# One-token attention and GeGLU on one core: TensorE's repeated halves as loops, and one chunk of rows dealt unevenly to the DMA engines

## The chip, the cores and the metric

The kernel runs on one core of a Trainium2 chip. The metric is device time in microseconds; lower is better.

## The reference

One decode step of a transformer block in float32: eight sequences, one new token each, model width 1024, 32 query heads of 128 on 4 key/value heads, a window of the last 1024 cached positions, and a gated MLP of width 3584.

```python
h  = x + attention(layernorm(x))          # q = x@wq; softmax(q k^T / sqrt(128)) v; @wo
g  = layernorm(h) @ w_gate                # [8, 3584]
u  = layernorm(h) @ w_up
h2 = h + (gelu(g) * u) @ w_down           # w_down is [3584, 1024]
```

Every weight and every cached key and value is used once, so nearly all of the 111 MB read are these.

## The kernel before

The weights go through one tile in on-chip memory, `w`, which has 2 x 16384 floats on each of 128 partitions: two halves of 8.39 MB (`HALF`, `PLACE`). They were laid out on the host in the order of use, one contiguous row for each partition and load. Only SyncE's queue loads them (`load`): each load waits on a semaphore until TensorE's last product has read the half that it overwrites, and while one half is being used the other is being filled. So the order of the loads is the order of the work: wq in two halves, k in two, v in two, wo in two, then w_gate and w_up (a first pair with four column blocks of 512, a second pair with three), then w_down.

Each stage multiplies by 32-column stationary tiles, so four products stand side by side in TensorE's four column groups. The activations are spread over the partitions for this, and VectorE transposes them between the stages.

- Attention: scores for both halves of heads first (L204), each with its softmax (L211 to L218) into tiles of its own; then, for each half, the transposes of the probabilities (L240), the product with v (L254) and the sum over the heads' own columns (L261, L264). `heads_out` turns this into the operand of wo (L225, L228).
- wo gives y (L281), which is folded by a product with `add2` (L291) and added to x (L296).
- Gate and up (L310), GELU (L334), product (L336), and a transposition into `at_`: on VectorE for the first 16 row blocks (L338), on TensorE for the other 12 (L342, L345).
- w_down: 28 rows of 128 x 1024, a row being 0.5 MB. They come in chunks of `DN_PARTS` rows (8, 8, 4, 4, 2, 1), and the last row in two parts (192 and 64 columns of each quarter). Rows 0 to 25 go into one accumulator (L364), on two column groups up to row `SLOW` and then on four. VectorE copies this out as `d1` (L371). Row 26 (L378), `d1` folded by `add2` (L384) and the parts of row 27 (L391) are summed in two more accumulators, and two additions with `h_sb` (L401, L404) give the output, which two DMAs store.

The chip has 16 DMA engines, and a load of 128 partitions is spread over all. The last part of row 27 is loaded as 100, 20 and 8 partitions (`SHARES`), so that some engines carry more of it than others.

Of the kernel before, what the change touches and what calls it, by code (L numbers as in the profile page):

```python
# [8 lines left out]
P = 128  # L9
# [17 lines left out]
ROUND = 3 * N * NC  # L27
PLACE = [0, HALF] * 5 + [0, ROUND]
DN_PARTS = (8, 8, 4, 4, 2, 1)
DN_AT = (2 * ROUND, 0, 8 * D, ROUND, ROUND + 4 * D, ROUND + 6 * D)  # L30

SHARES = ((0, 100), (100, 120), (120, 128))
LAST_AT = ROUND + 7 * D

SLOW = 20

# [41 lines left out]
def decode_block(nc, out, x, srcs, W):  # L78
# [13 lines left out]
    s_load = [nc.alloc_semaphore(f"s_load{i}") for i in range(len(srcs))]  # L92
    s_fin = nc.alloc_semaphore("s_fin")
# [5 lines left out]
    loaded[-1] = (s_load[-1], 16 * len(SHARES))  # L99
# [19 lines left out]
    qz = [sb(f"qz{hf}", [P, 2, 10 * 32]) for hf in range(2)]  # L119
    ot = sb("ot", [P, HQ, 32])  # L120
    for a in (*qz, ot):
        t_zero = pool(lambda e: e.memset(a, 0.0))
# [14 lines left out]
    def layernorm_t(src, name, *deps):  # L137
# [26 lines left out]
        t = dve(lambda e: e.transpose(xt.rearrange("p c m -> p (c m)"), xn), t)  # L164
        return xt, t
# [14 lines left out]
    for hf in range(2):  # L180
        load(2 + hf, PLACE[hf], HALF, t_q[hf])
    for hf in range(2):
        q_sb = sb(f"q{hf}", [P, N])
        t = dve(lambda e: e.tensor_scalar(q_sb, bank(4 + hf), scale, None, op0=ALU.mult), t_q[hf])  # L184
        qt = sb(f"qt{hf}", [P, N])
        t = dve(lambda e: e.transpose(qt, q_sb), t)
        for s in range(2):
            last = dve(lambda e: e.tensor_copy(
                qz[hf][:, s].rearrange("p (b m) -> p b m", b=B)[:, :, 0:REP],
                qt.rearrange("p (s k b r) -> p s b k r", s=2, k=REP, r=4)[:, s, :, :, 0]), t, t_zero)  # L190
        t_qz.append(last)


    t_s, t_p, share, t_share = [], [], [], []
    p_sb = [sb(f"p{hf}", [P, W]) for hf in range(2)]
    for hf in range(2):
        s_ps = bank(2 * hf, 2)
        k_t = w[:, hf * HALF:(hf + 1) * HALF].rearrange("p (s b k) -> p s b k", s=2, b=B)
        for b in range(HB):
            for k0 in range(0, W, N):  # L200
                for r in range(NQ):
                    s, half = divmod(r, 2)
                    at = 32 * b + 160 * half
                    ins = pe(lambda e: e.matmul(  # L204
                        s_ps[32 * r:32 * r + 32, k0:k0 + N], qz[hf][:, s, at:at + 32],
                        k_t[:, s, half * HB + b, k0:k0 + N],
                        start=(b == 0), stop=(b == HB - 1)), loaded[2 + hf], t_qz[hf], inc=False)
        t_s.append(pe.mark(ins))
        load(4 + hf, PLACE[hf], HALF, t_s[hf])
        nmax = sb(f"nmax{hf}", [P, 1])  # L210
        t = dve(lambda e: e.tensor_reduce(out=nmax, in_=s_ps, axis=AX.X, op=ALU.max, negate=True), t_s[hf])  # L211
        tot = sb(f"tot{hf}", [P, 1])
        t = act(lambda e: e.activation(p_sb[hf], s_ps, AF.Exp, bias=nmax, accum_out=tot), t)  # L213
        t_p.append(t)
        rtot = sb(f"rtot{hf}", [P, 1])
        t = dve(lambda e: e.reciprocal(rtot, tot), t)
        share.append(sb(f"share{hf}", [P, HB]))
        t_share.append(dve(lambda e: e.tensor_scalar(share[hf], own, rtot, None, op0=ALU.mult), t, t_own))  # L218


    t_o, o_sb, t_osb, t_ot = [], [], [], [None, None]

    def heads_out(hf, b, *deps):
        op = bank(b)[:, 0:P]
        t = pe(lambda e: e.transpose(op, o_sb[hf], ident), t_osb[hf], t_id, *deps)  # L225
# [6 lines left out]
    free = [None, None]  # L232
    for hf in range(2):
        pt = sb(f"pt{hf}", [P, KC, P])
        t_pt = []
        for h in range(2):
            pp = bank(6 + h).rearrange("p (c m) -> p c m", m=P)
            for i in range(KC // 2):
                c = h * KC // 2 + i
                ins = pe(lambda e: e.transpose(pp[:, i], p_sb[hf][:, c * P:(c + 1) * P], ident),  # L240
                         t_p[hf], t_id, free[h], inc=False)
            t = pe.mark(ins)
            dst = pt[:, h * KC // 2:(h + 1) * KC // 2, :]
            if h == 0:
                free[h] = dve(lambda e: e.tensor_copy(dst, pp), t)
            else:
                free[h] = act(lambda e: e.copy(dst, pp), t)
            t_pt.append(free[h])
        v_t = w[:, hf * HALF:(hf + 1) * HALF].rearrange("p (s c b d) -> p s c b d", s=2, c=KC, b=B)
        o_ps = bank(4 + hf)  # L250
        for c in range(KC):
            for r in range(NQ):
                s, half = divmod(r, 2)
                ins = pe(lambda e: e.matmul(  # L254
                    o_ps[32 * r:32 * r + 32, :], pt[:, c, 32 * r:32 * r + 32],
                    v_t[:, s, c, half * HB:(half + 1) * HB, :],
                    start=(c == 0), stop=(c == KC - 1)), loaded[4 + hf], t_pt[2 * c // KC], t_qz[hf], inc=False)
        t_o.append(pe.mark(ins))
        load(6 + hf, PLACE[hf], HALF, t_o[hf])
        o_sb.append(sb(f"o{hf}", [P, DH]))  # L260
        t = dve(lambda e: e.tensor_scalar(  # L261
            o_sb[hf], o_ps[:, 0:DH], share[hf][:, 0:1], None, op0=ALU.mult), t_o[hf], t_share[hf])
        for b in range(1, HB):
            t = dve(lambda e: e.scalar_tensor_tensor(  # L264
                o_sb[hf], o_ps[:, b * DH:(b + 1) * DH], share[hf][:, b:b + 1], o_sb[hf],
                op0=ALU.mult, op1=ALU.add), t)
        t_osb.append(t)
        if hf == 1:
            heads_out(0, 6, *free)
# [4 lines left out]
    for hf in range(2):  # L274
        if hf == 1:
            heads_out(1, 7, *free)
        for h in range(0, 2 * REP, 2):
            for r in range(NQ):
# [5 lines left out]
                    loaded[6 + hf], t_ot[hf], t_p[0], inc=False)  # L284
        t_y.append(pe.mark(ins))
        load(8 + hf, PLACE[hf], HALF, t_y[hf])
# [10 lines left out]
    ht, t_ht = layernorm_t(h_sb, "ln2", t_h)  # L297
# [3 lines left out]
    t_at = []  # L301
    for k, nb in enumerate((NQ, DF // N - NQ)):
        pair = bank(2 + 2 * k, 2)
        t_g = []
        for s in range(2):
            i = 8 + 2 * k + s
            for c in range(NC):
                for j in range(nb):
                    at = PLACE[i] + (c * nb + j) * N
                    ins = pe(lambda e: e.matmul(  # L310
                        pair[32 * j:32 * j + 32, s * N:(s + 1) * N], ht[:, c], w[:, at:at + N],
                        start=(c == 0), stop=(c == NC - 1)), loaded[i], t_ht, t_p[1], t_osb[1], inc=False)
                if k == 0 and s == 1 and c == NC // 2 - 1:
                    t_half = pe.mark(ins)
            t_g.append(pe.mark(ins))
            if k == 0 and s == 0:
                load(10, PLACE[10], ROUND, t_g[0])
            elif k == 0:
                load(11, PLACE[11], ROUND, t_half)
                load(12, DN_AT[0], DN_PARTS[0] * D, t_g[1])  # L320
            elif s == 0:
                for i in range(1, 3):
                    load(12 + i, DN_AT[i], DN_PARTS[i] * D, t_g[0])
            else:
                for i in range(3, len(DN_PARTS)):
                    load(12 + i, DN_AT[i], DN_PARTS[i] * D, t_g[1])
                load(tail, LAST_AT, NQ * CUT)
                at = LAST_AT + NQ * CUT
                for p0, p1 in SHARES:
                    nc.sync.dma_start(w[p0:p1, at:at + D - NQ * CUT], srcs[tail + 1][p0:p1]).then_inc(  # L330
                        s_load[tail + 1], 16)
        rows = 32 * nb
        ge = sb(f"ge{k}", [P, N])
        t = act(lambda e: e.activation(ge[:rows], pair[:rows, 0:N], AF.Gelu_apprx_tanh), t_g[0])  # L334
        hm = sb(f"hm{k}", [P, N])
        t = dve(lambda e: e.tensor_mul(hm[:rows], ge[:rows], pair[:rows, N:2 * N]), t, t_g[1])  # L336
        if k == 0:
            t_at.append(dve(lambda e: e.transpose(at_[:, 0:16, :].rearrange("p c m -> p (c m)"), hm), t))  # L338
        else:
            hp = bank(6)[:, 0:4 * rows].rearrange("p (i m) -> p i m", i=4)  # L340
            for i in range(4):
                ins = pe(lambda e: e.transpose(hp[:, i], hm[:rows, i * P:(i + 1) * P], ident[:rows, :rows]),  # L342
                         t, t_ot[0], inc=False)
            t = pe.mark(ins)
            t_at.append(dve(lambda e: e.tensor_copy(  # L345
# [139 lines left out]
```

## Time and profile before

| | |
|---|---|
| median of 3 runs | 265.94 us (265.69 to 267.08) |
| the profiled execution | 265.95 us, span 264.6 us |
| TensorE busy | 137.1 us (52%) |
| VectorE, ScalarE busy | 24.2 us, 10.2 us |
| read from HBM | 111.18 MB, 421 GB/s over the span |
| code packets of TensorE's queue | 7 of 16 KB |

The span runs from the first instruction to the last; the measured time has 1.35 us around it. Lines are L with a number of the kernel before. PE is TensorE's products, PEld its weight loads, DVE VectorE, ACT ScalarE, SP SyncE. In the timeline a row has its start, its length, the engine, the line, the operation with what it writes and reads, a count, and in brackets how long the engine had been idle and for what. In the chain a row has start, length and what ran. In the windows, the columns are the stretch, its length, busy time and count of each engine, the granted TensorE clock, the share of the 16 DMA engines that was busy, and GB/s. "instruction" in the DMA rows is code that an engine's sequencer fetches through the same DMA engines.

### The profile page before, as it was taken

To read this page: it belongs to the slowest core of one execution; us is meant where nothing else is said; L and a number is where in the kernel's file an instruction comes from. 1 tells how busy PE (TensorE), PEld (TensorE's weight loads), DVE (VectorE), ACT (ScalarE), POOL (GpSimd) and SP (SyncE) were. 2 spreads that over 40 slices of the span, in tenths; PEclk is the share of its full clock that TensorE was granted. 3 is DMA by queue.
4 is the path that set the end of the run, shared out by engine and by line. 5 is a ranking of instruction groups with operands and counts; after the bars stand their busy time and mean duration, and the time that the engine had idled before them with its cause. 6 is when DMAs were issued, how large, how long until landed. Compare 5 with 4: busy or idle time off the path is not lost.

```text
span 264.6 us, 1990 instructions
## 1 busy us (share of the span) xinstructions
PE 137.1 (52%) x918; PEld 38.1 (14%) x918; DVE 24.2 (9%) x74; ACT 10.2 (4%) x14; POOL 2.7 (1%) x9
## 2 busy tenths in 40 slices
PE   0005706705806906807707708509409485689795
PEld 0001201101201301202102102102102021122131
DVE  1050200200110020300200000330000200010001
ACT  1020000000010020110000000020000000000000
POOL 4000000000000000000000000000000000000000
PEclk9999975955965895965975956956965959599999
DMA  8997999899999999998999899989999999999994
GB/s 317 480 466 327 475 475 428 367 466 475 406 396 466 468 396 416 456 475 357 448 457 456 367 446 458 456 386 436 458 411 446 394 468 411 423 421 411 426 417 135
DMA packets 3236, 111.44 MB, mean 421 GB/s; under 512 B 508, under 2 KB 796, under 8 KB 1052
## 3 DMA queue, kind: packets, MB, share of 16 engines
q1 hardware_dynamic: 3036, 111.25, 97.8%
q8 instruction: 7, 0.11, 0.2%
q10 hardware_dynamic: 192, 0.07, 0.1%
q14 instruction: 1, 0.01, 0.0%
HBM read 111.18 MB, written 0.13 MB: 421 GB/s over the span
## 4 chain that ended last, share of the span: by engine, by line
DMA 78%; PE 21%; SPq 0%; issue 0%; DVE 0%
DMA w<-weights 78%; PE banks L310 6%; PE banks L204 4%; PE banks L175 4%; PE banks L254 4%; PE banks L281 3%; SPq L104 0%; PE banks L378 0%; PE banks L384 0%; PE banks L391 0%; DVE o_fin L401 0%; DVE o_fin L404 0%; PE banks L225 0%
## 5 line engine op out<-in xcount | busy, mean ns | idle before, releaser
L310 PE MATMUL banks<-w,ln_t 128*32 128x512 f32 x224 | 37.4, 751 | 29.2 <-DMA w<-weights 29.2
L175 PE MATMUL banks<-w,ln_t 128*32 128x512 f32 x128 | 18.2, 734 | 33.2 <-DMA w<-weights 33.2
L204 PE MATMUL banks<-w,qz 128*32 128x512 f32 x128 | 19.3, 770 | 21.2 <-DMA w<-weights 21.2
L281 PE MATMUL banks<-w,ot 128*32 128x512 f32 x128 | 18.4, 741 | 19.2 <-DMA w<-weights 19.2
L254 PE MATMUL banks<-w,pt 128*32 128x512 f32 x128 | 18.0, 727 | 18.1 <-DMA w<-weights 18.1
L364 PE MATMUL banks<-w,at 128*32 128x512 f32 x104 | 20.3, 595 | 2.2 <-DMA w<-weights 2.1
L310 PEld LDWEIGHTS banks<-w,ln_t 128*32 128x32 f32 x224 | 9.2, 134 | 56.9 <-issue 34.2
L175 PEld LDWEIGHTS banks<-w,ln_t 128*32 128x32 f32 x128 | 4.7, 132 | 45.8 <-issue 34.5
L204 PEld LDWEIGHTS banks<-w,qz 128*32 128x32 f32 x128 | 5.3, 137 | 35.2 <-issue 35.2
L281 PEld LDWEIGHTS banks<-w,ot 128*32 128x32 f32 x128 | 5.0, 132 | 31.2 <-issue 31.2
L254 PEld LDWEIGHTS banks<-w,pt 128*32 128x32 f32 x128 | 4.9, 131 | 29.8 <-issue 29.8
L364 PEld LDWEIGHTS banks<-w,at 128*32 128x32 f32 x104 | 5.3, 109 | 16.5 <-issue 12.3
L336 DVE TENSOR_TENSOR hm<-ge,banks 128x512 f32<-128x512 f32 (+1 forms) x2 | 1.4, 686 | 60.3 <-PE banks L310 60.3
L211 DVE TENSOR_REDUCE nmax<-banks 128x1 f32<-128x1024 f32 x2 | 2.5, 1225 | 35.7 <-PE banks L204 35.7
L213 ACT ACTIVATE p<-banks,nmax 128x1024 f32<-128x1024 f32 x2 | 2.2, 1114 | 75.8 <-DVE nmax L211 75.8
L184 DVE TENSOR_SCALAR q<-banks 128x512 f32<-128x512 f32 x2 | 1.4, 692 | 32.3 <-PE banks L175 32.3
L261 DVE TENSOR_SCALAR o<-banks,share 128x128 f32<-128x128 f32 x2 | 0.7, 351 | 32.6 <-PE banks L254 32.6
L148 ACT ACTIVATE ln_sd<-ln_ve 32x1 f32<-32x1 f32 x2 | 0.4, 202 | 70.5 <-DVE ln_ve L146 70.5
L334 ACT ACTIVATE ge<-banks 128x512 f32<-128x512 f32 (+1 forms) x2 | 1.2, 595 | 48.2 <-PE banks L310 48.2
L371 DVE COPY d<-banks 128x512 f32<-128x512 f32 x1 | 0.7, 692 | 22.0 <-PE banks L364 22.0
L148 ACT ACT_TABLE_LOAD x2 | 2.6, 1283 | 1.7 <-DVE add L125 1.7
L228 DVE COPY ot<-banks 128x64 f32<-128x64 f32 x4 | 0.8, 262 | 18.4 <-PE banks L225 18.4
(55 smaller groups left out, 34.2 us busy)
## 6 DMA issues: line engine op xcount, KB each, us to landing
w<-weights SPq DMA_DIRECT2D x2, 6144.0 KB, 23.5
w<-weights SPq DMA_DIRECT2D x2, 4096.0 KB, 26.7
w<-weights SPq DMA_DIRECT2D x2, 2048.0 KB, 24.6
w<-weights SPq DMA_DIRECT2D x1, 1024.0 KB, 22.3
w<-weights SPq DMA_DIRECT2D x1, 512.0 KB, 23.6
w<-weights SPq DMA_DIRECT2D x1, 384.0 KB, 24.0
w<-weights SPq DMA_DIRECT2D x10, 29.6
w<-weights SPq DMA_DIRECT2D x1, 100.0 KB
```

Of the source, the lines that this page charges most:

```text
L148: t = act(lambda e: e.activation(sd, ve, AF.Sqrt), t_ve)
L175: ins = pe(lambda e: e.matmul(q_ps[32 * j:32 * j + 32, :], xt[:, c], w[:, hf * HALF + c * SET + j * N:hf * HALF + c * SET + (j + 1) * N], ...
L184: t = dve(lambda e: e.tensor_scalar(q_sb, bank(4 + hf), scale, None, op0=ALU.mult), t_q[hf])
L204: ins = pe(lambda e: e.matmul(s_ps[32 * r:32 * r + 32, k0:k0 + N], qz[hf][:, s, at:at + 32], k_t[:, s, half * HB + b, k0:k0 + N], start=(b ...
L211: t = dve(lambda e: e.tensor_reduce(out=nmax, in_=s_ps, axis=AX.X, op=ALU.max, negate=True), t_s[hf])
L213: t = act(lambda e: e.activation(p_sb[hf], s_ps, AF.Exp, bias=nmax, accum_out=tot), t)
L254: ins = pe(lambda e: e.matmul(o_ps[32 * r:32 * r + 32, :], pt[:, c, 32 * r:32 * r + 32], v_t[:, s, c, half * HB:(half + 1) * HB, :], start ...
L281: ins = pe(lambda e: e.matmul(y_ps[32 * r:32 * r + 32, :], ot[:, 2 * hf * REP + h + e_], w[:, at:at + N], start=(hf == 0 and h == 0), stop ...
L310: ins = pe(lambda e: e.matmul(pair[32 * j:32 * j + 32, s * N:(s + 1) * N], ht[:, c], w[:, at:at + N], start=(c == 0), stop=(c == NC - 1)), ...
L334: t = act(lambda e: e.activation(ge[:rows], pair[:rows, 0:N], AF.Gelu_apprx_tanh), t_g[0])
L336: t = dve(lambda e: e.tensor_mul(hm[:rows], ge[:rows], pair[:rows, N:2 * N]), t, t_g[1])
L364: ins = pe(lambda e: e.matmul(d1_ps[32 * r:32 * r + 32, :], at_[:, q, :], w[:, at:at + N], start=(r not in started), stop=(q >= pairs - 2) ...
```

## The change

1. On TensorE, attention becomes a loop that runs twice over one piece of code (`nc.Fori` on that engine alone): scores, transposes, product with v. The order of the loads becomes k, v, k, v. Semaphores that the loop waits on are counted down by each wait (`take`), and the tiles `qz`, `p`, `pt` and the accumulators exist once in place of twice. `heads_out` for both halves follows behind the loop.
2. Gate and up likewise: two rounds with four column blocks of 448 each (`M`, `SIDE`). VectorE does both transpositions.
3. w_down's chunks are 8, 8, 4, 3, 1, 2, 1 rows. The chunk of one row (`SHARED`, row 23) is loaded by three DMAs over 32, 60 and 36 partitions, whose source has an outer dimension of 16, 10 and 9: nine engines get 12 rows of 4 KB, one 8 and six 2. The last part of row 27 is one load.
4. The tail: `d1` holds rows 0 to 23 (`QUADS`); `d1`, folded, and rows 24 to 26 are summed in one accumulator, which VectorE adds to `h_sb` as `pre`; row 27's parts have accumulators of their own, added to `pre`.
5. Behind TensorE's last product stand two instruction blocks, each aligned to 256 instructions and holding one no-op.

```diff
-PLACE = [0, HALF] * 5 + [0, ROUND]
-DN_PARTS = (8, 8, 4, 4, 2, 1)
-SHARES = ((0, 100), (100, 120), (120, 128))
+M = DF // (2 * NQ)
+SIDE = NC * NQ * M
+PLACE = [0, HALF] * 6
+DN_PARTS = (8, 8, 4, 3, 1, 2, 1)
+SHARED = 4
+SHARES = ((16, 2), (10, 6), (9, 4))
 SLOW = 20
+QUADS = 24
...
+    def take(sem, n):
+        nc.tensor.wait_ge(sem, n).then_inc(sem, -n)
+    with nc.Fori(0, 2, 1, engines=[nc.tensor.engine]):
+        take(s_qz, 1)
+        take(s_k, 16)
...
+                    ins = nc.tensor.matmul(
+                        s_ps[32 * r:32 * r + 32, k0:k0 + N], qz[:, s, at:at + 32],
+                        k_t[:, s, half * HB + b, k0:k0 + N],
+                        start=(b == 0), stop=(b == HB - 1))
+        ins.then_inc(pe.sem, 1)
+        take(s_p, 1)
...
+        take(s_v, 16)
...
+    for hf in range(2):
+        t_s, t_pp0, t_pp1, t_o = marks[hf]
...
+        load(4 + 2 * hf, PLACE[4 + 2 * hf], HALF, t_s)
...
+        load(5 + 2 * hf, PLACE[5 + 2 * hf], HALF, t_o)
...
+    heads_out(0, 6)
+    heads_out(1, 7)
...
+    with nc.Fori(0, 2, 1, engines=[nc.tensor.engine]):
+        take(s_free, 1)
+        for s, sem in enumerate((s_g, s_u)):
+            take(sem, 16)
...
+        for (n, each), src in zip(SHARES, srcs[12 + i]):
+            nc.sync.dma_start(w[src[0]:src[0] + n * each, at:at + D], src[1]).then_inc(s_load[12 + i], 16)
...
+    for j in range(NQ):
+        pe(lambda e: e.matmul(
+            bank(0)[32 * j:32 * j + 32, 0:QW], add2[:, j // 2, :], d1[:, (j % 2) * QW:(j % 2) * QW + QW],
+            start=True, stop=False), t_d1, inc=False)
+    for q in range(QUADS, rows - 1):
...
+    t_pre = dve(lambda e: e.tensor_add(pre, h_sb, bank(0)[:, 0:QW]), t)
+    fin = [(1, 0, CUT), (4, CUT, QW - CUT)]
...
+    for _ in range(2):
+        nc.tensor.addr_align(256, 0)
+        nc.tensor.nop(nofuse=True)
```

TensorE's code from the scores to wo, before. A row has its line, the operation, the tile that it writes and those it reads, the shape and a count of equal rows; `x64` at L204 is both halves of the scores:

```order
L204 MATMUL banks<-w,qz 32x512 x64
L240 MATMUL banks<-ident,p 128x128 x8
L254 MATMUL banks<-w,pt 32x512 x32
L240 MATMUL banks<-ident,p 128x128 x8
L254 MATMUL banks<-w,pt 32x512 x32
L225 MATMUL banks<-ident,o 128x128
L281 MATMUL banks<-w,ot 32x512 x32
```

The same place after the change; a row of a loop stands once and runs twice:

```order
L207 UNCONDITIONAL_BRANCH
L215 MATMUL banks<-w,qz 32x512 x32
L224 MATMUL banks<-ident,p 128x128 x8
L232 MATMUL banks<-w,pt 32x512 x32
L207 REGISTER_ALU
L207 COMPARE_AND_BRANCH
L244 MATMUL banks<-ident,o 128x128 x2
L293 MATMUL banks<-w,ot 32x512 x64
```

The second half of the scores now comes behind the first product with v, and both transposes of `o` stand ahead of all of wo.

TensorE's code at the end, before, from w_down on:

```order
L364 MATMUL banks<-w,at 32x512 x52
L378 MATMUL banks<-w,at 32x192 x4
L378 MATMUL banks<-w,at 32x64 x4
L384 MATMUL banks<-d,add 32x192 x4
L384 MATMUL banks<-d,add 32x64 x4
L391 MATMUL banks<-w,at 32x192 x4
L391 MATMUL banks<-w,at 32x64 x4
```

And after, `d` being `d1`:

```order
L375 MATMUL banks<-w,at 32x512 x48
L385 MATMUL banks<-d,add 32x256 x4
L392 MATMUL banks<-w,at 32x256 x12
L404 MATMUL banks<-w,at 32x192 x4
L404 MATMUL banks<-w,at 32x64 x4
L411 ISA x2
```

The folding of `d1` has moved ahead of three rows of w_down; before, it stood behind row 26. Rows 24 and 25 have left the large accumulator.

More of the change, by code (lines that the diff above doesn't have):

```diff
@@ L179, in decode_block @@
         t_q.append(pe.mark(ins))
-    for hf in range(2):
-        load(2 + hf, PLACE[hf], HALF, t_q[hf])
+    load(2, PLACE[2], HALF, t_q[0])
+    load(3, PLACE[3], HALF, t_q[1])
+    qt = []
     for hf in range(2):
@@ L209, in decode_block @@
[L209 to L218, printed above, removed]
@@ L221, in decode_block @@
-    t_o, o_sb, t_osb, t_ot = [], [], [], [None, None]
-    def heads_out(hf, b, *deps):
+                        start=(b == 0), stop=(b == HB - 1))
+        ins.then_inc(pe.sem, 1)
+        take(s_p, 1)
+        for h in range(2):
+            for i in range(KC // 2):
+                c = h * KC // 2 + i
+                ins = nc.tensor.transpose(pp[h][:, i], p_sb[:, c * P:(c + 1) * P], ident)
+            ins.then_inc(pe.sem, 1)
+        take(s_v, 16)
+        for c in range(KC):
+            if 2 * c % KC == 0:
+                take(s_pt[2 * c // KC], 1)
+            for r in range(NQ):
+                s, half = divmod(r, 2)
+                ins = nc.tensor.matmul(
+                    o_ps[32 * r:32 * r + 32, :], pt[:, c, 32 * r:32 * r + 32],
+                    v_t[:, s, c, half * HB:(half + 1) * HB, :],
+                    start=(c == 0), stop=(c == KC - 1))
@@ L224, in heads_out @@
+        ins.then_inc(pe.sem, 1)
+    marks = [[(pe.sem, pe.n + 4 * hf + i + 1) for i in range(4)] for hf in range(2)]
+    pe.n += 8
+    o_sb, t_osb, t_ot = [], [], [None, None]
+    def heads_out(hf, b):
         op = bank(b)[:, 0:P]
-        t = pe(lambda e: e.transpose(op, o_sb[hf], ident), t_osb[hf], t_id, *deps)
+        t = pe(lambda e: e.transpose(op, o_sb[hf], ident), t_osb[hf])
         for s in range(2):
@@ L230, in heads_out @@
                 op[:, 64 * s:64 * s + 64].rearrange("p (b h) -> p h b", h=REP)), t, t_zero)
-    free = [None, None]
     for hf in range(2):
[L234 to L259, printed above, removed]
@@ L296, in decode_block @@
     t_h = dve(lambda e: e.tensor_add(h_sb, x_sb, yy), t)
-    ht, t_ht = layernorm_t(h_sb, "ln2", t_h)
+    ht, _ = layernorm_t(h_sb, "ln2", t_h, sem=s_free)
     at_ = sb("at", [P, DF // P, 32])
[L301 to L306, printed above, removed]
-            for c in range(NC):
[L308 to L336, printed above, removed]
@@ new lines, in decode_block, with load_rows @@
+    marks = [[(pe.sem, pe.n + 2 * k + s + 1) for s in range(2)] for k in range(2)]
+    pe.n += 4
+    place, of = [], []
+    for i, n in enumerate(DN_PARTS):
+        for _ in range(n):
+            place.append(len(place) * D)
+            of.append(12 + i)
+    def load_rows(i, *deps):
+        at = place[of.index(12 + i)]
+        if i != SHARED:
+            load(12 + i, at, DN_PARTS[i] * D, *deps)
+            return
+        sp.wait(*deps)
+        for (n, each), src in zip(SHARES, srcs[12 + i]):
+            nc.sync.dma_start(w[src[0]:src[0] + n * each, at:at + D], src[1]).then_inc(s_load[12 + i], 16)
@@ L337, in decode_block @@
+    for k in range(2):
+        t_g, t_u = marks[k]
         if k == 0:
-            t_at.append(dve(lambda e: e.transpose(at_[:, 0:16, :].rearrange("p c m -> p (c m)"), hm), t))
-        else:
[L340 to L345, printed above, removed]
-                at_[:, 16:28, :].rearrange("p (j i) m -> p i j m", j=nb),
-                hp.rearrange("p i (j m) -> p i j m", j=nb)), t))
@@ L350, in decode_block @@
-    where = []
-    for n, at in zip(DN_PARTS, DN_AT):
-        where += [(at + i * D, len(where)) for i in range(n)]
-    of = []
-    for i, n in enumerate(DN_PARTS):
-        of += [12 + i] * n
+            load(10, PLACE[10], SIDE, t_g)
+            load(11, PLACE[11], SIDE, t_u)
+        else:
+            for i in range(2):
+                load_rows(i, t_g)
+            for i in range(2, len(DN_PARTS)):
+                load_rows(i, t_u)
+            last = (DF // P - 1) * D
+            load(tail, last, NQ * CUT)
+            load(tail + 1, last + NQ * CUT, D - NQ * CUT)
@@ L359, in decode_block @@
     started = set()
-    for q in range(pairs):
+    for q in range(QUADS):
         for ch in range(2):
             r = ch if q < SLOW else 2 * (q % 2) + ch
-            at = where[q][0] + ch * N
+            at = place[q] + ch * N
             ins = pe(lambda e: e.matmul(
                 d1_ps[32 * r:32 * r + 32, :], at_[:, q, :], w[:, at:at + N],
-                start=(r not in started), stop=(q >= pairs - 2)),
-                loaded[of[q]], t_at[0 if q < 16 else 1], t_ot[1], inc=False)
+                start=(r not in started), stop=(q >= QUADS - 2)),
+                loaded[of[q]], t_at if q >= half else None, t_ot[1], inc=False)
```

168 lines of the change are left out of this document (101 added, 67 removed).

## The prediction

> **What bounds the kernel now.** I read the page first: its shares of the chain, its DMA rows, its busy times.
>
> ```profile
> PE 137.1 (52%) x918; PEld 38.1 (14%) x918; DVE 24.2 (9%) x74; ACT 10.2 (4%) x14; POOL 2.7 (1%) x9
> GB/s 317 480 466 327 475 475 428 367 466 475 406 396 466 468 396 416 456 475 357 448 457 456 367 446 458 456 386 436 458 411 446 394 468 411 423 421 411 426 417 135
> q8 instruction: 7, 0.11, 0.2%
> HBM read 111.18 MB, written 0.13 MB: 421 GB/s over the span
> DMA 78%; PE 21%; SPq 0%; issue 0%; DVE 0%
> ```
>
> The weights stream from the first slice to the last but one; TensorE works half of the time. The chain in order of time says whether the stream ever stops:
>
> ```profile
> 81.99 9.97 PE banks L204 x64
> 91.98 28.69 DMA w<-weights
> 120.80 9.30 PE banks L254 x64
> 130.16 29.35 DMA w<-weights
> ```
>
> A load is issued at 91.98 and has landed 28.69 us later, at 120.67; the next one on the chain lands at 130.16 + 29.35 = 159.51. Between them lie two loads of 8.39 MB, so one takes 38.84 / 2 = 19.4 us, or 432 GB/s. Of the 28.69 us, 28.7 - 19.4 = 9.3 us are time in which the load only queued behind the one before it. So the stream does not stop, and TensorE can be 9.3 us late with a half of `w` before it does. The PE shares in the chain are a path through the graph, not time that a faster TensorE would return.
>
> The end is different. I asked the timeline for the last rows of w_down, and the windows for how the stream runs out:
>
> ```profile
> 246.75 13.36 PE L364 MATMUL banks<-w,at 128*32 128x512 f32 x72 [2.13 <-DMA w<-weights]
> 257.44 1.52 PE L364 MATMUL banks<-w,at 128*32 128x512 f32 x10
> 257.87 1.09 PE L364 MATMUL banks<-w,at 128*32 128x512 f32 x6
> 259.04 0.16 PEld L364 LDWEIGHTS banks<-w,at 128*32 128x32 f32 x8 [0.99 <-DMA w<-weights]
> 260.17 0.69 DVE L371 COPY d<-banks 128x512 f32<-128x512 f32 x1 [21.95 <-PE banks L364]
> 260.82 0.64 PE L378 MATMUL banks<-w,at 128*32 128x192 f32 x16 [0.72 <-DMA w<-weights]
> 261.28 0.62 PE L384 MATMUL banks<-d,add 128*32 128x192 f32 x16
> 262.18 0.16 PEld L391 LDWEIGHTS banks<-w,at 128*32 128x32 f32 x8 [0.29 <-DMA w<-weights]
> 262.33 0.35 DVE L401 TENSOR_TENSOR o_fin<-h_sb,banks 128x192 f32<-128x192 f32 x1 [1.47 <-PE banks L391]
> ```
>
> From 246.75, when rows 8 to 15 have landed, TensorE runs row after row without a gap up to row 23, whose products end at 257.87 + 1.09 = 258.96; the second and the third of these timeline rows are the same run seen from two later windows, and they differ by 4 MATMULs, one row, and 257.87 - 257.44 = 0.43 us. Then it waits for data three times: 259.04 for rows 24 and 25, 260.82 for row 26, 262.18 for the last part of row 27. So the end hangs on landings by tenths of a microsecond, with a TensorE that is nearly as late.
>
> ```profile
> 258.00:259.00 1.00, 0.96 (x10) 0.05 (x2) 0.00 (x0) 0.00 (x0) 0.00 (x0) 1.00 0.98 386
> 259.00:259.50 0.50, 0.46 (x6) 0.16 (x8) 0.00 (x0) 0.00 (x0) 0.00 (x0) 1.00 1.11 320
> 259.50:260.00 0.50, 0.50 (x8) 0.00 (x0) 0.00 (x0) 0.00 (x0) 0.00 (x0) 1.00 0.57 164
> 260.00:260.50 0.50, 0.10 (x4) 0.00 (x0) 0.33 (x1) 0.00 (x0) 0.00 (x0) 1.00 0.44 150
> 260.50:261.00 0.50, 0.18 (x4) 0.16 (x8) 0.36 (x1) 0.00 (x0) 0.00 (x0) 1.00 0.33 123
> 261.00:261.50 0.50, 0.50 (x24) 0.42 (x20) 0.00 (x0) 0.00 (x0) 0.00 (x0) 1.00 0.07 23
> q8 instruction: 1, 0.02, 2.5%
> ```
>
> The last two columns but one are the granted clock (1.00) and the share of the 16 DMA engines that is busy: 0.57, 0.44, 0.33, 0.07 in half microseconds. The engines run out over 2 us, not together. The last row is the DMA view for 259 to 262: one code packet of TensorE fell into these 3 us and took 2.5% x 16 x 3 = 1.2 us of one engine. The seven of the page give the same: 0.2% x 16 x 264.6 / 7 = 1.2 us each. A code packet makes one engine late by 1.2 us for all that follows, and a load has landed only when the latest engine has.
>
> **The change, part by part.**
>
> *Attention in the order K0, V0, K1, V1.* New is that the softmax now stands between two halves. The groups of instructions give its price:
>
> ```profile
> L211 DVE TENSOR_REDUCE nmax<-banks 128x1 f32<-128x1024 f32 x2 | 2.5, 1225 | 35.7 <-PE banks L204 35.7
> L213 ACT ACTIVATE p<-banks,nmax 128x1024 f32<-128x1024 f32 x2 | 2.2, 1114 | 75.8 <-DVE nmax L211 75.8
> L240 PE MATMUL banks<-ident,p 128*128 128x128 f32 x16 | 2.2, 279 | 0.0
> L245 DVE COPY pt<-banks 128x512 f32<-128x512 f32 x2 | 1.4, 682 | 0.0
> ```
>
> Scores 9.97, maximum 1.23, exponential 1.11, reciprocal and share about 0.6 (an estimate, small operations between the two), eight transposes 2.2 / 2 = 1.1, copy 0.68: 14.7 us after K0 has landed TensorE is ready for V0, which lands 19.4 us after K0. Hidden, with 4.7 us over. The loads still go to the two halves in turn, each issued when its half has been used up. heads_out for both halves now stands ahead of wo; it ran beside V1's stream, now beside wo's, with some 9 us of cover. Cost nothing.
>
> *The loops.* They shorten TensorE's code. The page has 918 + 918 instructions for 7 code packets, 262 for each. After the change the code holds 128 + 136 + 2 + 128 + 8 + 128 + 96 + 8 + 24 + 16 = 674 MATMULs (a product of the order listing is two, a transpose one) and as many weight loads, 1348 instructions, 5.1 packets; what is executed is 1876, or 7.2 packets. If a block that is run again is still there, five packets fall before the last product, and the two aligned blocks behind it bring two more, outside the stream. If it is not, there are 7 or more in the stream. The jump back itself waits for nothing: it comes 9.3 us before the next half lands (8 us in the second loop, whose loads are 7/8 as long). Nor does the second loop's `s_free` cost anything: gelu, product and transpose, an estimated 2 us (three operations of about the copy's 0.68), lie in that same gap.
>
> [...]
>
> *GeGLU in four equal sides.* 128 products of 448 columns in place of 112 of 512: the same 57,344 columns, the same bytes ahead of the last side, so that it still lands where TensorE starts on it now:
>
> ```profile
> 227.33 8.94 PE L310 MATMUL banks<-w,ln_t 128*32 128x512 f32 x48 [5.16 <-DMA w<-weights]
> ```
>
> Its products (by columns 448 x 32 / (512 x 24) = 1.17 times as many) end near 237, when rows 0 to 7 land. Cost nothing; the transposes of L342 go.
>
> *The shared chunk.* 16 x 2 + 10 x 6 + 9 x 4 rows: nine engines carry 12 rows of 4 KB, one 8, six 2, where an even split is 8. An engine moves 432 / 16 = 27 GB/s, so 4 rows more are 0.6 us, 6 fewer are 0.9 us less: 1.5 us between the two groups, against a packet's 1.2. Levelled fully, the stream's rest after 259.0 is 0.5 x (1.0 + 0.57 + 0.44 + 0.33 + 0.07) = 1.2 us (the 1.11 taken as full), so it ends at 260.2 in place of about 261.3: 1.1 us earlier, if the six are the late ones. This is the gain on offer. With the code packet at 259 gone too, all landings of the end move by about that much: row 26 to below 260, the last part of row 27 from 262.18 to about 261.1.
>
> *The tail on TensorE.* It cannot use all of this. Row 8 still starts with the landing at 246.75, since one late engine is enough for that, and rows 8 to 23 take the same time, to 258.96. Then, in a row:
>
> ```profile
> 168.37 0.69 DVE L288 COPY y_sb<-banks 128x512 f32<-128x512 f32 x1 [17.58 <-PE banks L281]
> 169.11 0.64 PE L291 MATMUL banks<-y_sb,add 128*32 128x256 f32 x8 [0.81 <-DVE y_sb L288]
> 169.82 0.42 DVE L296 TENSOR_TENSOR h_sb<-x_sb,banks 128x256 f32<-128x256 f32 x1 [0.76 <-PE banks L291]
> ```
>
> These are the same operations in the same shapes as the new end. d1's copy starts 0.07 behind the last product, 259.03, and takes 0.69; the four products of L385 start 0.05 later, 259.77. They and the twelve of L392 (rows 24 to 26, landed by then, but queued behind L385) are four times 0.43 us, with 0.64 - 0.43 = 0.21 for the last to run out: 261.70. `pre` starts 0.07 later and takes 0.42, to 262.19; the first final add takes 0.35, to 262.54. Row 27's products run beside `pre`. Before, that add ended at 262.33 + 0.35 = 262.68. So the end comes 0.14 us earlier: the wait for row 27 goes, and late next is the copy of d1, since three rows now stand behind it where one stood ahead of it.
>
> **The sum.** The profiled execution took 265.95 us with a span of 264.6 (1.35 around it), and the median of the runs shown is 265.94, so nothing needs shifting. 265.95 - 0.15 = 265.8. The DMA side alone would give 265.95 - 1.1 = 264.85; the rows on TensorE are nearer, so I take these.
>
> **The rivals.** (1) *The stream sets the end after all, and it is earlier.* If rows 8 to 15 land sooner, the whole TensorE end moves with them. At most the packet's 1.2 us: 264.6. For it speaks that fewer packets lie ahead of row 15; against it, that a single late engine holds the landing where it is. 0.12, more than half of it under the bound below. (2) *One more code packet on an engine that is late already* moves that landing by 1.2: 267.0. 0.10. (3) *The loops fetch their code again*, at both jumps, and two of the packets meet an engine that carries one: rows 8 to 15 land 2.4 us later, 265.8 + 2.4 = 268.2, slower. It decides as soon as row 8 starts behind 248.3, since up to 1.5 us more stay within the bound. [...] 0.10. (4) *The aligned blocks* are fetched at 262 and later, just when the output goes out; a packet ahead of it on its engine costs up to 1.2: 266.4 to 267.0. The room is this landing time of now, the last number of the row:
>
> ```profile
> out<-o_fin SPq DMA_DIRECT2D x1, 96.0 KB, 1.7
> ```
>
> Or the blocks aren't fetched before the kernel's end, and cost nothing. 0.08.
>
> **How the numbers follow.** The forecast has 0.60: 265.8, with 265.4 to 266.1 for the small terms. The range goes down into rival 1 and up through 2 and 4, 264.8 to 267.1; it leaves out rival 3 and the lower part of rival 1. A measurement of this kernel can tell about 0.5% (1.33 us) from no change: faster is under 264.6, slower over 267.3. Faster: 0.08, of rival 1. Slower: rival 3 and some of 2 and 4 on top of another, 0.15. Within: 0.77.
>
> **What would show it.** Right: row 8 starts near 246.7; `d`'s copy near 259.0, with L385, L392 and `pre` behind it without a DMA wait; the busy share of the DMA engines falls from full to nothing within about 1 us, before 261; first final add near 262.2. Code packets within the stream: 5. Wrong: L404 waiting for data at the end (the shares miss the late engines); row 8 behind 248 or 8 and more code packets (rival 3); a first row 8 ahead of 246 (rival 1); output landings later than 1.7 us after their issue (rival 4); a gap in the chain between loads, which would mean that a half was used up over 9 us late.

## Result and profile after

| | before | after |
|---|---|---|
| median | 265.98 us (265.69 to 267.08) | 273.86 us (273.09 to 274.78) |
| span of the profiled execution | 264.6 us | 272.7 us |
| first final addition starts | 262.33 | 265.41 |
| code packets of TensorE's queue | 7 | 5 |

The changed kernel is slower: 1.0287 times the time before, 95% interval 1.0251 to 1.0323. The execution that was profiled is the slowest of the four after (274.78 us). Its span grew by 8.1 us, in two places that have nothing to do with each other.

From the page after, the row of GB/s in 40 slices of 6.8 us and the row of TensorE's code packets:

```profile
GB/s 308 466 461 462 404 365 464 452 462 461 317 462 452 454 462 404 385 452 452 463 452 337 461 406 505 412 404 429 474 429 412 429 412 437 433 416 413 257 201 19
q8 instruction: 5, 0.08, 0.1%
```

The stream holds its rate for 37 slices, and the code came in five packets, not more. Then come two slices at 257 and 201 GB/s, where before there was one at 135. The windows of that stretch, first of after, then of before (columns as in the prediction):

```profile
250.00:253.50 3.50, 3.50 (x18) 0.93 (x16) 0.00 (x0) 0.00 (x0) 0.00 (x0) 1.00 1.03 408
253.50:256.00 2.50, 2.50 (x14) 0.70 (x12) 0.00 (x0) 0.00 (x0) 0.00 (x0) 1.00 0.98 213
256.00:258.00 2.00, 2.00 (x16) 0.62 (x14) 0.00 (x0) 0.00 (x0) 0.00 (x0) 1.00 1.04 223
258.00:260.30 2.30, 0.92 (x8) 0.01 (x3) 0.00 (x0) 0.00 (x0) 0.00 (x0) 1.00 0.93 281
```

```profile
253.50:256.00 2.50, 2.50 (x14) 0.70 (x12) 0.00 (x0) 0.00 (x0) 0.00 (x0) 1.00 0.92 387
256.00:258.00 2.00, 2.00 (x20) 0.70 (x18) 0.00 (x0) 0.00 (x0) 0.00 (x0) 1.00 0.99 407
258.00:260.30 2.30, 2.02 (x18) 0.21 (x10) 0.13 (x1) 0.00 (x0) 0.00 (x0) 1.00 0.85 292
```

The share of busy DMA engines is the same, about 1, and the bytes are half. The engines do not wait for work; each packet takes longer: in the traces, the median packet of 4 KB between 253.5 and 258 took 305 ns after and 160 ns before. From 253.5 to 260.3, after moved 213 x 2.5 + 223 x 2.0 + 281 x 2.3 = 1625 KB, before 2453 KB: 828 KB behind, or 2.0 us at 410 GB/s.

TensorE and VectorE in the timeline after:

```profile
246.70 12.21 PE L375 MATMUL banks<-w,at 128*32 128x512 f32 x60 [0.95 <-DMA w<-weights]
260.29 1.05 PE L375 MATMUL banks<-w,at 128*32 128x512 f32 x4 [1.38 <-DMA w<-weights]
262.14 0.64 PE L385 MATMUL banks<-d,add 128*32 128x256 f32 x8 [0.79 <-DVE d L382]
262.59 1.82 PE L392 MATMUL banks<-w,at 128*32 128x256 f32 x24
264.74 0.64 PE L404 MATMUL banks<-w,at 128*32 128x192 f32 x16 [0.32 <-DMA w<-weights]
265.05 0.17 PEld L404 LDWEIGHTS banks<-w,at 128*32 128x32 f32 x8 [0.16 <-DMA w<-weights]
```

```profile
261.39 0.69 DVE L382 COPY d<-banks 128x512 f32<-128x512 f32 x1 [25.00 <-PE banks L375]
265.41 0.35 DVE L417 TENSOR_TENSOR o_fin<-pre,banks 128x192 f32<-128x192 f32 x1 [0.50 <-PE banks L404]
265.68 0.21 DVE L420 TENSOR_TENSOR o_fin<-pre,banks 128x64 f32<-128x64 f32 x1
```

Row 8 starts at 246.70. Up to row 22 all is as forecast; then TensorE waits 1.38 us for row 23, the shared chunk, which it gets at 260.29. The copy of `d1`, forecast at 259.03, starts at 261.39. Row 27 is late as well: L404 waits for its first part at 264.74 and for its last part at 265.05. The last addition ends at 265.68 + 0.21 = 265.89; before, by the same view, it ended at 262.82. That is **3.07 us**.

The output goes out at 265.8 and 266.0 and takes 1.6 us (DMA view of after, issue to landing):

```profile
out<-o_fin SPq DMA_DIRECT2D x1, 96.0 KB, 1.6
out<-o_fin ACTq DMA_DIRECT2D x1, 32.0 KB, 1.6
```

So it has landed at 267.6, but the span goes on to 272.65. What runs there is a view of one line, the aligned blocks (engine, operation, count, duration in ns, first and last start in us):

```profile
L411 PEldq NOP  x105: 13/13/13, 265.1 to 272.6; - x105
```

105 no-ops, one every 7.5 us / 104 = 72 ns, from TensorE's last product to the end of the span. At most two are the kernel's own; the others can only be the fill up to the next multiple of 256 instructions, and TensorE goes through them one by one. In the second block the fill has up to 255 places, yet no more no-ops are recorded. They delay nothing of the work, but the kernel ends when its last engine does: 272.65 - 267.6 = **5.0 us**. 3.07 + 5.0 is the whole of the 8.1.

The span isn't quite all. At about 273.9 us, behind the last no-op on record, the DMA view shows one more packet of TensorE's code, and this execution took 2.1 us more than its span (274.78 - 272.65), where before it was 1.35. What TensorE did in that time is not on record.

### The profile page after: what moved, and what is told of

The parts are those of the page before. It is cut to its first block, busy times and chain, and to the rows that moved or that the text cites. A ratio compares the mean times of both kernels' runs of the same rounds, so it can differ in the third digit from the quotient of the medians.

```text
span 272.7 us, 2159 instructions
## 1 busy us (share of the span) xinstructions
PE 134.8 (49%) x938; PEld 39.2 (14%) x938; DVE 24.6 (9%) x75; ACT 10.2 (4%) x14; POOL 2.2 (1%) x8
## 5 line engine op out<-in xcount | busy, mean ns | idle before, releaser
L321 PE MATMUL banks<-w,ln_t 128*32 128x448 f32 x256 | 32.0, 662 | 32.1 <-PEq L204 32.1
L182 PE MATMUL banks<-w,ln_t 128*32 128x512 f32 x128 | 17.5, 708 | 33.5 <-DMA w<-weights 33.5
L293 PE MATMUL banks<-w,ot 128*32 128x512 f32 x128 | 19.4, 772 | 18.4 <-DMA w<-weights 18.4
L375 PE MATMUL banks<-w,at 128*32 128x512 f32 x96 | 22.0, 633 | 4.3 <-DMA w<-weights 4.3
L321 PEld LDWEIGHTS banks<-w,ln_t 128*32 128x32 f32 x256 | 9.9, 130 | 53.8 <-issue 53.8
L182 PEld LDWEIGHTS banks<-w,ln_t 128*32 128x32 f32 x128 | 4.6, 128 | 45.6 <-issue 33.8
L359 DVE TENSOR_TENSOR hm<-ge,banks 128x448 f32<-128x448 f32 x2 | 1.2, 622 | 57.9 <-PE banks L321 57.9
L224 PE MATMUL banks<-ident,p 128*128 128x128 f32 x16 | 3.0, 350 | 6.3 <-PEq L204 6.3
L300 DVE COPY y_sb<-banks 128x512 f32<-128x512 f32 x1 | 0.7, 692 | 37.4 <-PE banks L293 37.4
L224 PEld LDWEIGHTS banks<-ident,p 128*128 128x128 f32 x16 | 2.4, 182 | 8.0 <-issue 8.0
```

What stands on the lines that cost most here:

```text
L182: ins = pe(lambda e: e.matmul(q_ps[32 * j:32 * j + 32, :], xt[:, c], w[:, hf * HALF + c * SET + j * N:hf * HALF + c * SET + (j + 1) * N], ...
L224: ins = nc.tensor.transpose(pp[h][:, i], p_sb[:, c * P:(c + 1) * P], ident)
L293: ins = pe(lambda e: e.matmul(y_ps[32 * r:32 * r + 32, :], ot[:, 2 * hf * REP + h + e_], w[:, at:at + N], start=(hf == 0 and h == 0), stop ...
L321: ins = nc.tensor.matmul(bank(2 + s)[32 * j:32 * j + 32, 0:M], ht[:, c], w[:, at:at + M], start=(c == 0), stop=(c == NC - 1))
L375: ins = pe(lambda e: e.matmul(d1_ps[32 * r:32 * r + 32, :], at_[:, q, :], w[:, at:at + N], start=(r not in started), stop=(q >= QUADS - 2) ...
```

## Experiments

The theory: the no-ops cost 5.0 us and the shared chunk 3.1; loops, sides and the order of the tail cost nothing. The rivals stand in the expectations. All of these kernels compute the whole of the reference.

### Without the aligned blocks

```diff
-    for _ in range(2):
-        nc.tensor.addr_align(256, 0)
-        nc.tensor.nop(nofuse=True)
```

> The changed kernel without the two aligned blocks behind TensorE's last product. Theory: the output has landed at 267.6 in the changed kernel's trace, and 105 no-ops that fill the first block up to its edge run on TensorE until 272.65; they hold the program's end. Then this gives 272.7 - 5.0 = 267.7 of span, about 268.9 us. Rival: the no-ops are an appearance of the profile and the program's end waits for something else; then 273.9 as the changed kernel. A second rival: the blocks keep code packets on the same DMA engines from one execution to the next; then times without them scatter by 1 to 2 us more than with them.

268.85 us (268.07 to 269.19), 1.0093 (1.0063 to 1.0123) of before; the span ends at 267.9, with the output. The 5.0 us are the blocks. The times do not scatter more without them (1.1 us from lowest to highest, 1.7 with them), so the second rival falls too. The rest of the loss is untouched: the last addition ends at 266.1.

### The blocks alone, on the kernel before

```diff
         t = pe.mark(ins)
+    for _ in range(2):
+        nc.tensor.addr_align(256, 0)
+        nc.tensor.nop(nofuse=True)
```

> The kernel before with the same two aligned blocks behind its last product. Theory: no-ops up to the next edge of 256 instructions run behind the last product at 72 ns each. Its code ends elsewhere in its block, so their number differs: if it is about 100 as in the changed kernel, TensorE ends near 270 and the time is 5 us more, about 271; if the fill is jumped over there, the time stays at 266. Rival, by which the blocks cost nothing in any kernel: 266.

273.68 us (273.57 to 273.92), 1.0286 (1.0261 to 1.0311). The same view of the blocks' line:

```profile
L398 PEldq NOP  x137: 13/13/13, 262.1 to 272.1; - x137
```

The additions are where they were before (262.3 to 262.8); 137 no-ops at 73 ns follow TensorE's last product, and the kernel is 7.7 us longer. I had expected about 100 of them and 5 us. If the fill is the distance to the next edge, any change of the code's length changes its price: 137 here, 105 in after, and 105 again below in the kernel with the blocks and a plain chunk, whose code on TensorE is as long. No run moves the edge by a known number of instructions.

### Without the shared chunk, and without both

```diff
-SHARED = 4
+SHARED = -100
```

Row 23 is then loaded like all others. With the blocks kept:

> The changed kernel with row 23 loaded by one load of 128 partitions, the blocks kept. Theory: the three loads of 32, 60 and 36 partitions crowd the DMA engines (busy 1.0, 213 to 223 GB/s from 253.5 to 258, where 410 is usual); without them row 23 is there when TensorE comes to it at 257.9, and the last addition ends near 262.7 in place of 265.9. The no-ops then still run 7.6 us: span near 269.6, about 270.8 us. Rival: the new order of the tail (d1's copy ahead of three rows) is what is late; then the last addition stays above 264.5 and the time above 272.5.

And without them:

> The changed kernel without the blocks and with row 23 in one plain load: what is left are the loops, the equal sides and the new tail. If the two theories hold and add up, the last addition ends near 262.7 and the output lands near 264.5: about 265.8 us, as the kernel before. If the loops or the tail cost something of their own: 267 or more.

Without both: 266.03 us (265.76 to 267.61), 1.0011 (0.9988 to 1.0034). Everything else in the change, taken together, costs nothing that can be measured, and gains nothing. The end of this kernel, TensorE and then VectorE:

```profile
247.04 12.21 PE L374 MATMUL banks<-w,at 128*32 128x512 f32 x64 [2.65 <-DMA w<-weights]
260.08 0.64 PE L384 MATMUL banks<-d,add 128*32 128x256 f32 x8 [0.83 <-DVE d L381]
260.53 1.48 PE L391 MATMUL banks<-w,at 128*32 128x256 f32 x24
261.83 0.62 PE L403 MATMUL banks<-w,at 128*32 128x192 f32 x16
```

```profile
259.33 0.69 DVE L381 COPY d<-banks 128x512 f32<-128x512 f32 x1 [22.08 <-PE banks L374]
262.53 0.35 DVE L413 TENSOR_TENSOR o_fin<-pre,banks 128x192 f32<-128x192 f32 x1
```

Nothing waits for a DMA after row 8. This is the chain of the prediction, every step of it 0.3 us later because row 8 starts 0.3 later: copy 259.33 (forecast 259.03), fold 260.08 (259.77), first addition 262.53 (262.19).

With the blocks kept: 272.35 us (271.49 to 272.64), 1.0226 (1.0195 to 1.0257). That is 1.5 more than expected. Its last additions lie at 264.1 to 264.6, 1.6 us behind the kernel without both, although the loads are the same. In the profiled execution the timeline shows the place, and the windows the cause (the granted clock is the last column but two):

```profile
246.95 13.91 PE L374 MATMUL banks<-w,at 128*32 128x512 f32 x64 [2.65 <-DMA w<-weights]
```

```profile
246.90:248.00 1.10, 1.05 (x4) 0.33 (x6) 0.00 (x0) 0.00 (x0) 0.00 (x0) 0.57 1.01 432
248.00:250.00 2.00, 2.00 (x6) 0.37 (x4) 0.00 (x0) 0.00 (x0) 0.00 (x0) 0.50 0.99 418
250.00:252.00 2.00, 2.00 (x10) 0.54 (x8) 0.00 (x0) 0.00 (x0) 0.00 (x0) 0.88 1.01 428
```

The same window of the kernel without both:

```profile
248.00:250.00 2.00, 2.00 (x12) 0.51 (x10) 0.00 (x0) 0.00 (x0) 0.00 (x0) 1.00 0.95 403
```

After the same idle time of 2.65 us, one kernel got half the clock for some 3 us, and 6 MATMULs in place of 12 in two of them; the other got the full clock. 13.91 - 12.21 = 1.7 us of a TensorE that has nothing to spare here. For the three other runs of this kernel there is no profile. It isn't a cost of the plain chunk: of the profiles below that have this idle time, one shows half the clock (0.52 after 2.65 us) and three the full one (1.00 after 2.65, 2.66 and 2.66 us).

### What makes the shared chunk slow

The theory was at first that the unequal shares stretch the packets: nine engines with six times the rows of the six others. An even split into the same three loads:

```diff
-SHARES = ((16, 2), (10, 6), (9, 4))
+SHARES = ((16, 2), (16, 4), (16, 2))
```

> The changed kernel without the blocks, with row 23 in three loads of 32, 64 and 32 partitions, each over 16 engines: 8 rows for every engine, in the same padded source. Theory of crowded destinations: 16 engines write into the same 32 partitions at once; packets of 4 KB take 200 to 400 ns where 159 is usual, and row 23 lands near 259 or later. Theory of unequal work (12 rows on nine engines take longer): even shares land like the plain load, near 256.9. Theory of the source's layout: slow here, and slow in the next kernel too.

One load of all 128 partitions, from the padded source, which has an outer dimension of 16:

```diff
+SHARES = ((16, 8),)
```

> As e5, but row 23 is one load of 128 partitions from the same padded source (16 blocks of 8 rows). Theory of crowded destinations: near the plain load, row 23 landed by 257.5, time near 266.3. Theory of the source's layout: as slow as e5 and the changed kernel, row 23 at 259 or later.

And unequal shares from an ordinary source, in the three loads that the kernel before uses for its last part (the edit is against the kernel without both):

```diff
+SHARED = 4
+SHARES = ((0, 100), (100, 120), (120, 128))
...
+            nc.sync.dma_start(w[p0:p1, at:at + D], srcs[12 + i][p0:p1]).then_inc(s_load[12 + i], 16)
...
```

> e3 (no blocks, plain rows) with row 23 in three loads of 100, 20 and 8 partitions of the ordinary layout, the shares that the kernel before gives to its last quarter row: 10 engines carry 12 or 13 rows of 4 KB, six none. Theory of crowded destinations: the ten engines write to partitions 10e to 10e+9, mostly apart; little stretching, the stream levelled, its last landing near 261.2 (e3: 261.9), and with TensorE as in e3 the same 266.0 us. Theory of unequal work or of several loads by themselves: row 23 lands 2 us late as in the changed kernel, 268.5.

None of the three has the blocks. Measured: even thirds 267.54 us (266.92 to 267.74), 1.0047 (1.0028 to 1.0066); one padded load 267.93 (267.87 to 268.4), 1.0065 (1.0046 to 1.0084); ordinary source in 100, 20 and 8 partitions 269.0 (267.62 to 269.12), 1.0085 (1.0054 to 1.0116). Their windows, in this order:

```profile
253.50:256.00 2.50, 2.50 (x16) 0.65 (x12) 0.00 (x0) 0.00 (x0) 0.00 (x0) 1.00 0.99 259
256.00:258.00 2.00, 2.00 (x16) 0.66 (x14) 0.00 (x0) 0.00 (x0) 0.00 (x0) 1.00 1.02 315
```

```profile
253.50:256.00 2.50, 2.50 (x14) 0.70 (x12) 0.00 (x0) 0.00 (x0) 0.00 (x0) 1.00 1.03 206
256.00:258.00 2.00, 1.94 (x16) 0.39 (x12) 0.00 (x0) 0.00 (x0) 0.00 (x0) 1.00 0.98 238
```

```profile
253.50:256.00 2.50, 2.50 (x14) 0.68 (x12) 0.00 (x0) 0.00 (x0) 0.00 (x0) 1.00 1.04 241
256.00:258.00 2.00, 2.00 (x14) 0.61 (x14) 0.00 (x0) 0.00 (x0) 0.00 (x0) 1.00 0.99 197
```

All three are slow, with DMA engines that are busy throughout. My expectations for the last two missed: a single load with equal shares halves the stream just as well, and so do three loads of an ordinary source. So neither the inequality nor the padding nor the number of loads is needed for it. (The last kernel also ran at a clock of 0.52 from 246.7 to 250.0, so part of its 269.0 is not the loads'.) What is left is the order of the pieces: which rows are read and which partitions written at the same time. In none of the three is row 23 cut up as in a plain load.

### Two other mappings, measured in the middle of the stream

The kernel before, with three of its 8.39 MB halves loaded in another way: the second of k as two loads of 64 partitions, the second of v as one load of 16 blocks of 8 partitions, the second of wo as one load of 32 blocks of 4, these two from a padded source.

```diff
+BLOCKS = {5: 16, 7: 32}
...
+        if i == 3:
+            for p in (0, 64):
+                nc.sync.dma_start(w[p:p + 64, at:at + size], srcs[i][p:p + 64]).then_inc(s_load[i], 16)
+            return
...
```

> The kernel before, in which three of its eight-megabyte loads are shaped otherwise, each between ordinary ones that take 19.4 us: the second half of k as two loads of 64 partitions (ordinary source rows); the second half of v as one load of 128 partitions from a source of 16 blocks of 8 rows, the blocks set apart by an empty row as in the changed kernel; the second half of wo likewise from 32 blocks of 4 rows. Theory of crowded destinations (a group of partitions can take only its own part of the 433 GB/s, whichever engines write it): 64 partitions at a time halve the rate, 2 x 19.4 = 38.7 us for that load; the 16 blocks of 8, in which engine e writes partitions 8e to 8e+7, are slow too, up to 38.7. Theory of the source's layout: the two loads of 64 take 19.4 together, the padded ones are slow. Theory that only small packets suffer: all three 19.4.

One run, 314.18 us. Each half of `w` makes TensorE start when it has landed; the starts in the timeline and the windows of four stretches:

```profile
64.54 9.23 PE L211 MATMUL banks<-w,qz 128*32 128x512 f32 x64 [13.89 <-DMA w<-weights]
105.58 9.19 PE L211 MATMUL banks<-w,qz 128*32 128x512 f32 x64 [31.81 <-DMA w<-weights]
129.10 9.38 PE L261 MATMUL banks<-w,pt 128*32 128x512 f32 x64 [13.30 <-DMA w<-weights]
168.00 8.71 PE L261 MATMUL banks<-w,pt 128*32 128x512 f32 x64 [28.50 <-DMA w<-weights]
187.10 9.39 PE L288 MATMUL banks<-w,ot 128*32 128x512 f32 x64 [10.14 <-DMA w<-weights]
206.46 9.09 PE L288 MATMUL banks<-w,ot 128*32 128x512 f32 x56 [9.71 <-DMA w<-weights]
```

```profile
82.00:102.00 20.00, 0.00 (x0) 0.00 (x0) 0.00 (x0) 0.00 (x0) 0.00 (x0) 0.50 0.95 210
123.00:160.00 37.00, 10.40 (x72) 3.45 (x72) 2.00 (x5) 1.87 (x2) 0.00 (x0) 0.64 0.96 198
164.00:182.00 18.00, 8.96 (x65) 2.53 (x65) 1.71 (x6) 0.00 (x0) 0.00 (x0) 0.78 0.98 409
184.00:201.00 17.00, 9.65 (x65) 2.68 (x65) 0.40 (x2) 0.00 (x0) 0.00 (x0) 0.70 1.00 432
```

The two loads of 64 partitions took 105.58 - 64.54 = 41.0 us, at 210 GB/s; the 16 blocks of 8 took 168.00 - 129.10 = 38.9 us, at 198 GB/s; an ordinary load 19.1 us at 409 GB/s; the 32 blocks of 4, with the same kind of padded source, 19.4 us at 432 GB/s. The GB/s are those of a window near the middle of each load, not its bytes over its time. With DMA engines just as busy, the rate depends by a factor of two on how a load is cut into pieces. Partitions written at the same time are one reading. That the pieces lie differently in HBM as well, so that the reading side is slow, is not excluded for the 16 blocks. Which of the two it is, and what sets 16 blocks of 8 apart from 32 blocks of 4, was not shown: no run has on record which engine carries which block, though the expectation took block e for engine e.

### The fast mapping in the place of the slow one

```diff
+SHARES = ((32, 4),)
```

Row 23 as one padded load in 32 blocks of 4, otherwise the kernel without the aligned blocks.

> The shared chunk as one load of 128 partitions from the padded source, in 32 blocks of 4 partitions in place of the 16 blocks of 8 (267.93 us); no aligned blocks. Everything else as there. If the order in which the engines write the partitions is what halves the stream, this load costs what a plain one costs: 266.0 us (0.996 to 1.003 of the kernel before), row 23 landed near 257, over 390 GB/s from 253.5 to 258. If one padded load of 0.5 MB is slow for its source, its size or its place between two larger loads, it stays with the 16 blocks: 267.5 to 268.0, row 23 near 259.7, 210 to 240 GB/s in that stretch.

```profile
253.50:256.00 2.50, 2.50 (x14) 0.70 (x12) 0.00 (x0) 0.00 (x0) 0.00 (x0) 1.00 1.00 411
256.00:258.00 2.00, 2.00 (x20) 0.60 (x18) 0.00 (x0) 0.00 (x0) 0.00 (x0) 1.00 0.99 408
```

```profile
246.75 12.21 PE L375 MATMUL banks<-w,at 128*32 128x512 f32 x64 [2.66 <-DMA w<-weights]
```

411 and 408 GB/s in place of 206 and 238, the median packet of 4 KB back at 159 ns, and no wait for row 23. The ratio is 1.0019 (0.9997 to 1.004), against 1.0065 for the 16 blocks. Its median of 266.65 us lies between six times of 265.83 to 266.04 and six of 267.26 to 267.68; the upper group has no profile, but the kernel without both, which has no shared chunk at all, has three of ten there too (267.45 to 267.61). So the cut into blocks is the cause, shown at the place itself for one load; for the three loads of the change (32, 60 and 36 partitions, each on a part of the partitions) it is inferred from this and from the 64 partitions.

### Smaller chunks

The idle time of TensorE before row 8 can go if rows 8 to 15 come in two chunks. On the kernel without both:

```diff
-DN_PARTS = (8, 8, 4, 3, 1, 2, 1)
+DN_PARTS = (8, 4, 4, 4, 3, 1, 2, 1)
```

> e3 with rows 8 to 15 in two chunks of four. Theory: in e3 the end is a run on TensorE that starts with the landing of rows 8 to 15 (247.0); rows 8 to 11 land near 242, so TensorE goes on from row 7 without waiting and is then held by landings alone: d1's copy starts near 257.8 in place of 259.3, and the last addition near 262.0 (row 27's last part has landed at 261.9) in place of 262.5: 265.5 us. Rival: TensorE's run doesn't matter, the end is that of the stream: 266.0 as e3.

265.72 us (265.56 to 266.41), 0.9983 (0.9967 to 0.9999) of before: the fastest version, though the gain of 0.3 us is under what a reader should build on.

```profile
239.69 11.33 PE L374 MATMUL banks<-w,at 128*32 128x512 f32 x52
251.78 6.01 PE L374 MATMUL banks<-w,at 128*32 128x512 f32 x32 [0.77 <-DMA w<-weights]
261.47 0.64 PE L403 MATMUL banks<-w,at 128*32 128x192 f32 x16 [0.35 <-DMA w<-weights]
```

TensorE works through rows 0 to 15, to 239.69 + 11.33 = 251.02, waits 0.77 us for row 16 and is early now, so the end is set by the last landing: L403 waits for data. The shares of the kernel before on this last quarter row, 100, 20 and 8 partitions, were to bring that landing forward:

```diff
-            load(tail + 1, last + NQ * CUT, D - NQ * CUT)
+            for p0, p1 in ((0, 100), (100, 120), (120, 128)):
...
```

> e8 with the last quarter row in 100, 20 and 8 partitions, as in the kernel before, where 10 engines carry 12 or 13 of its 1 KB rows. In e8 the last five engines land 1.2 us behind the others (260.9 to 261.7 against 259.8 to 260.2) and the last addition waits for them. The pieces are 1 KB, so crowding costs at most some tenths. Last landing then that of row 27's first part, 261.4, last addition near 261.9 in place of 262.14: 265.5 us against e8's 265.7. Rival: the crowding or the two further loads eat the 0.3: 265.7 to 266.

265.96 us (265.89 to 266.36), 0.9985 (0.9968 to 1.0001). No gain: in the profiles the first final addition starts at 262.50 with the shares and at 262.14 without.

## Why the prediction was wrong

**The aligned blocks, rival 4: the failed step that cost 5.0 us.** I priced their code packets and nothing else, at 0 to 1.2 us. The fill ahead of an aligned block was code that TensorE executed, 105 instructions at 72 ns = 7.6 us, of which the landing of the output hid 2.5. The order of instructions showed `L411 ISA x2` and no fill, and the word "aligned" should have raised the question of what stands in the gap. The time is in the span's end and nowhere else, so that every row of the forecast's chain could hold and the total still be off. Of the two packets of the forecast one came, behind the span.

**The shared chunk: the failed step that cost 3.1 us.** "An engine moves 432 / 16 = 27 GB/s" took an engine's rate as its own, whatever the others write. The runs show 197 to 315 GB/s from 253.5 to 258 with row 23 in three or one badly cut loads, all engines busy, and 408 to 411 in the well-cut one. From this step came the gain on offer, 1.1 us earlier; the trace had 2.9 us later for the last part of row 27 (its weight loads at 265.05, against 262.18 before). With it fell "rows 8 to 23 take the same time, to 258.96": row 23 ended at 260.29 + 1.05 = 261.34. Nor were the engines levelled: the sixteen shares of row 27's last load landed between 261.75 and 265.01, and between 259.69 and 261.89 without the shared chunk. The range reached down for the levelling of the shares, and had nothing above for a load that costs more time in all.

**The loops, rival 3 and rival 2: not what happened.** Five code packets in the stream, the number of the forecast for code that stays where it is: both loops ran twice, and none was added. How long a body may be before its code has to come again is not shown: the two here have 272 and 256 matmul instructions, against the forecast's 262 to a packet, and no run has a longer one.

**The tail and row 8: right.** Row 8 at 246.70, as forecast (246.75 before), and rows 8 to 22 at the forecast's pace. Without the shared chunk the copy, fold, three rows and additions came with the forecast's lengths, and the end there was TensorE's and VectorE's chain, not a landing. This part alone gave 266.03 us for a forecast of 265.8.

**Attention's order, the four equal sides: right, at nothing.** The kernel that keeps them has the ratio 1.0011 (0.9988 to 1.0034).

## What to carry to other kernels

A DMA split can change not only how much each engine carries but how fast its packets go: try the split with one load in the middle of a stream, and look at GB/s beside the busy share, since a share of 1.0 at half the GB/s means that each packet takes twice as long (305 ns in place of 160 here). Ask of padding that an assembler puts into code whether it is executed: here it was, and behind the last product it is paid for as soon as it outlasts the output. When adding up a change, ask for each engine when it stops, not only when the output is written.

## What was not expected of the hardware

- A load of all 128 partitions runs at 432 GB/s in 32 blocks of 4 partitions and at 198 GB/s in 16 blocks of 8; the DMA engines look equally busy (1.00 and 0.96).
- A no-op of TensorE's fill takes 72 to 73 ns from one to the next, though its own record is 13 ns long.
- Half the clock for some 3 us after an idle time of 2.65 us, in some executions and not in others (0.50 and 1.00 between 248 and 250), worth 1.7 us here. The kernel without that idle time, with the smaller chunks, had ten runs within 0.9 us; the kernel before, with 2.13 us of it, has some a full microsecond above its median. That these runs had half the clock is not shown.
